# Order of one quarter's modulation columns, and of two loads, at the head of an adaLN linear-attention and GeGLU block

## The chip, the cores and the metric

The kernel runs on one core of one Trainium2 chip. The metric is the device time of one execution in microseconds (us); lower is better. The kernel before takes 838.47 us in the median of its first three runs (838.35 to 839.31).

PE is TensorE, PEld its weight loads, DVE is VectorE, ACT is ScalarE, POOL is GpSimd and SP is SyncE, whose queue issues almost all loads.

## The reference

One transformer block on 2048 tokens of width 1024, in bf16. A conditioning vector `c` makes six modulation vectors. The first two, a shift `sa` and a scale `ca`, are applied to the layer-normalized tokens before the QKV product:

```python
mod = (_silu(c) @ w_mod).reshape(c.shape[0], 6, 1, -1)
sa, ca, ga, sb, cb, gb = ...
h = _layernorm(x) * (1 + ca) + sa
x = x + ga * linear_attention(h, wqkv, wo)     # phi(t) = (t > 0 ? t + 1 : exp(t)) + 1e-6, 32 heads
h = _layernorm(x) * (1 + cb) + sb
x = x + gb * ((gelu(h @ w_gate) * (h @ w_up)) @ w_down)
```

Before any K matmul of a row block of `wk` can run, the matching part of `sa` and `ca` must have been multiplied out, for which 4 MB of `w_mod` are loaded. That head of the kernel is all that matters here.

## The kernel before

Tokens come in chunks of 128. The first four chunks are normalized on DVE (`ln1_bn`, `ln1_fin`, `xhat_dve`), transposed on PE (`t1`) and written to `h1T` by ACT. The modulation is worked out in four quarters of 256 columns; a quarter has two loads of 512 KB, its shift half (t = 0) and its scale half (t = 1). `mod_cols` turns them into four columns of PSUM, with 16 one-column matmuls for a half; `mod_copy` moves them to `modt`; `mod1` applies them to `h1T` on DVE. Then the K matmuls of the two rows of `wk` that belong to the quarter can run.

```python
def wmq_dma(q, ts=(0, 1)):           # shift half first, then scale half
    for t in ts:
        sch.dma(Q, ... WMQ[q][:, :, t, :] <- wm_v[:, :, t * D + q * 256:t * D + (q + 1) * 256] ...)

# the loads, all on SP's queue, in this order
x_dma(0, 1); x_dma(1, 2)
wmq_dma(0, (1,))
x_dma(2, 3)
wmq_dma(0, (0,))
x_dma(3, 4)
w_dma(WK, OFF_WK, "wk", 1, 0, D, 0, 2)               # wk rows 0-1
for q in range(1, 4):
    wmq_dma(q)
    for d0, d1 in ((2, 4),) if q == 1 else ((2 * q, 2 * q + 1), (2 * q + 1, 2 * q + 2)):
        w_dma(WK, OFF_WK, "wk", 1, 0, D, d0, d1)     # wk rows 2-3, 4, 5, 6, 7
w_dma(WV, ...)                                       # ... wv, tokens 4-7, wq

def mod_cols(q, bank, ts=(1, 0)):    # scale columns first, then shift columns
    for t in ts:
        ...                          # 16 matmuls 128x1 for each half

# PE's program order at the head (DVE's parts between)
warm(11, 7); t1(0, 5); warm(6, 7); mod_cols(0, 4); t1(1, 6)
mod_copy(0, 4); mod1(0, 1, 0, 2)
warm(4, 7)                           # matmuls on zeros, filler
k_part(0, [0])                       # K of chunk 0, rows 0-1
xhat_dve(2, ...); t1(2, 7); mod1(1, 1, 0, 2)
ln1_bn(3, 0); ln1_bn(3, 1); ln1_fin(3)
k_part(0, [1])
mod1(2, 1, 0, 2)
mod_cols(1, 4, (1,))                 # quarter 1, scale
k_part(0, [2])                       # K of chunk 2
xhat_dve(3, ...)
mod_cols(1, 4, (0,))                 # quarter 1, shift
mod_copy(1, 4); t1(3, 7); mod1(0, 3, 2, 4)
k_tiles([2, 3], ...)                 # "the next K matmuls": rows 2-3
...
mod_cols(2, 4); mod_copy(2, 4)       # quarter 2
... rows 4-5 ...
mod_cols(3, 4); mod_copy(3, 4)       # quarter 3
... rows 6-7, then the V matmuls (wv)
```

Every operation carries its own waits; an engine runs its list strictly in this order. So a wait of PE for one operand holds all PE work behind it (in the first timeline below, K matmuls that were ready near 15.0 us run at 15.94, behind a wait that ended at 15.52).

Of the kernel before, what the change touches and what calls it, by code (L numbers as in the profile page):

```python
# [12 lines left out]
D = 1024  # L13
# [32 lines left out]
OFF_WK = OFF_WD  # L46
# [168 lines left out]
def bass_adaLN_cond__linear_attn_block__geglu_ffn__prompt_kernel(  # L215
# [15 lines left out]
    with ExitStack() as es:  # L231
# [6 lines left out]
        def at(name, shape, dty, off):  # L238
            return nc.alloc_sbuf_tensor_at(name, shape, dty, offset=ABASE + off, align_bytes=4)
# [10 lines left out]
        WK = at("wk", [P, NDC, D], bf16, OFF_WK)  # L250
# [66 lines left out]
        def r_sm(name):  # L317
            return [(SMO[name], SMO[name] + SMSZ[name], name)]
# [7 lines left out]
        def r_xs(c0, c1):  # L326
            return [(OFF_XALL + c0 * D * 2, OFF_XALL + c1 * D * 2, "xall")]
# [13 lines left out]
        def r_w(off, name, dc, c0=0, c1=D):  # L341
            return [(off + (dc * D + c0) * 2, off + (dc * D + c1) * 2, name)]
# [14 lines left out]
        def r_wmq(i, t):  # L357
            return [(MSO[i] + (dc * 2 + t) * 512, MSO[i] + (dc * 2 + t + 1) * 512, f"wmq{i}") for dc in range(NDC)]
# [33 lines left out]
        def pr(b):  # L392
            return [(b * 2048, (b + 1) * 2048)]

        def PS(b, c0=0, c1=512):
            return ps_all[:, b * 512 + c0: b * 512 + c1]
# [44 lines left out]
        def x_dma(c0, c1):  # L441
            return sch.dma(Q, lambda e: e.dma_start(XALL[:, c0:c1, :], x_v[:, c0:c1, :]), wr=r_xs(c0, c1), note=f"x{c0}")  # L442
# [4 lines left out]
        def w_dma(dst, off, name, kind, c0, c1, dc0=0, dc1=NDC):  # L447
            return sch.dma(Q, lambda e: e.dma_start(dst[:, dc0:dc1, c0:c1], wqkv_v[:, dc0:dc1, kind * D + c0:kind * D + c1]),
                           wr=[t_ for dc in range(dc0, dc1) for t_ in r_w(off, name, dc, c0, c1)], note=f"{name}.{dc0}.{c0}")

        def wmq_dma(q, ts=(0, 1)):
            for t in ts:
                sch.dma(Q, lambda e, t=t: e.dma_start(WMQ[q][:, :, t, :], wm_v[:, :, t * D + q * 256:t * D + (q + 1) * 256]),  # L453
                        wr=r_wmq(q, t), note=f"wmq{q}.{t}")
# [6 lines left out]
        wmq_dma(0, (1,))  # L461
        x_dma(2, 3)
        wmq_dma(0, (0,))
        x_dma(3, 4)
        w_dma(WK, OFF_WK, "wk", 1, 0, D, 0, 2)
        for q in range(1, 4):
            wmq_dma(q)
            for d0, d1 in ((2, 4),) if q == 1 else ((2 * q, 2 * q + 1), (2 * q + 1, 2 * q + 2)):
# [35 lines left out]
        def xhat_dve(c_, dst, rng):  # L504
            sch.op(V, lambda e: e.tensor_scalar(dst[:, :], XALL[:, c_, :], MVA[:, c_, 0:1], RSA[:, c_:c_ + 1],  # L505
                                                op0=ALU.subtract, op1=ALU.mult),
                   rd=r_x(c_) + r_smc("mv", c_, 8) + r_smc("rs", c_, 4), wr=rng, note=f"xhat {c_}")
# [21 lines left out]
        def xh_buf(c_):  # L529
            i = c_ % 3  # L530
            return XH[i], r_2k(XHO[i], f"xh{i}")
# [52 lines left out]
        def mod1(c0, n, dc0=0, dc1=NDC):  # L584
            sg, ci = divmod(c0, CPG)
            mods(H1, r_h1, sg, sc1, ci * P, (ci + n) * P, dc0, dc1, "h1")
# [8 lines left out]
        def mod_cols(q, bank, ts=(1, 0)):  # L595
            o = None
            rng = [(bank * 2048 + (MC0 + q * 4) * 4, bank * 2048 + (MC0 + q * 4 + 4) * 4)]
            for t in ts:
                for b in range(2):
                    col = MC0 + q * 4 + t * 2 + b  # L600
                    for dc in range(NDC):
                        o = sch.op(T, lambda e, t=t, b=b, dc=dc, col=col: e.matmul(  # L602
                            PS(bank, col, col + 1), WMQ[q][:, dc, t, b * P:(b + 1) * P], SILUT[:, dc:dc + 1],
                            start=(q == b == dc == 0 and t == 1), stop=(dc == NDC - 1), skip_group_check=True),
                            rd=r_wmq(q, t) + r_sm("siluT"), pwr=(rng if dc == 0 else ()), note=f"mod{q}.{t}.{b}.{dc}")
            for t_ in rng:
                sch.ps.set_writer(t_[0], t_[1], o)

        def mod_copy(q, bank):
            rng = [(bank * 2048 + (MC0 + q * 4) * 4, bank * 2048 + (MC0 + q * 4 + 4) * 4)]  # L610
            sch.op(V, lambda e: e.tensor_tensor(MODT[:, q * 4:q * 4 + 4], PS(bank, MC0 + q * 4, MC0 + q * 4 + 4), ADD4[:, :], ALU.add),
                   prd=rng, rd=r_sm("add4"), wr=r_smc("modt", q, 16), note=f"modcp{q}")
# [121 lines left out]
        def warm(n, bank=None):  # L734
            for _ in range(n):
                sch.op(T, lambda e: e.matmul(PS(0 if bank is None else bank), WARM[:, 0:P], WARM[:, :], start=bank is not None,
                                             stop=bank is not None, skip_group_check=True),
                       rd=R_WARM, pwr=pr(bank) if bank is not None else (), note="warm")
# [29 lines left out]
        def k_part(q, cs):  # L768
            for dc in (2 * q, 2 * q + 1):
                for (c_, jg), b in kb0.items():  # L770
                    if c_ in cs:
                        kv_mm(c_, "k", jg, b, [dc])
                if 3 in cs:
                    k31([dc])
# [17 lines left out]
        ln1_fin(2)  # L792
        mod_copy(0, 4)
        mod1(0, 1, 0, 2)
        warm(4, 7)
        k_part(0, [0])
        xhat_dve(2, *xh_buf(2))
        t1(2, 7)
# [3 lines left out]
        ln1_fin(3)  # L802
        k_part(0, [1])
        mod1(2, 1, 0, 2)
        mod_cols(1, 4, (1,))
        k_part(0, [2])
        xhat_dve(3, *xh_buf(3))
        mod_cols(1, 4, (0,))
        mod_copy(1, 4)
        t1(3, 7)  # L810
        mod1(0, 3, 2, 4)
# [505 lines left out]
```

## Time and profile before

The page of the kernel before says that PE is busy almost all the time, at full granted clock:

```profile
span 836.2 us, 11354 instructions
PE 829.1 (99%) x4190; PEld 384.3 (46%) x4190; DVE 512.3 (61%) x898; ACT 336.3 (40%) x555; POOL 37.5 (4%) x91
```

The list of PE's waits has four entries (columns: who waited, for whom, us in total, how many times, the longest):

```profile
PE ps_all L478 <- POOL bmask L429: 2.1, 1, 2.1
PE ps_all L602 <- DMA wmq<-in_w_mod_dram: 1.9, 2, 1.0
PE ps_all L680 <- DMA wk<-in_A_wqkv_dram: 0.4, 1, 0.4
PE ps_all L680 <- DVE h1T L565: 0.2, 1, 0.2
```

They all lie before 18.1 us. L602 is `mod_cols`, L680 the K and V matmuls, L565 `mod1`. From there to the end PE waits for nothing, so an advance at the head is kept to the end, if no later load takes it back.

The PE timeline of the kernel before shows the place in question (columns: start, duration, engine, line, operation, tiles and shapes, count, and the idle time before with what ended it):

```profile
12.21 1.02 PE L680 MATMUL ps_all<-wk,h1T 128*128 128x512 bf16 x4 [0.36 <-DMA wk<-in_A_wqkv_dram]
13.07 0.61 PE L546 MATMUL ps_all<-ident,xh 128*128 128x128 bf16 x8
13.52 1.03 PE L680 MATMUL ps_all<-wk,h1T 128*128 128x512 bf16 x4
15.52 0.55 PE L602 MATMUL ps_all<-siluT,wmq 128*128 128x1 bf16 x16 [0.98 <-DMA wmq<-in_w_mod_dram]
15.94 1.02 PE L680 MATMUL ps_all<-wk,h1T 128*128 128x512 bf16 x4
16.80 0.54 PE L602 MATMUL ps_all<-siluT,wmq 128*128 128x1 bf16 x16
18.01 2.55 PE L680 MATMUL ps_all<-wk,h1T 128*128 128x512 bf16 x11 [0.20 <-DVE h1T L565]
21.45 0.94 PE L602 MATMUL ps_all<-siluT,wmq 128*128 128x1 bf16 x32
25.27 0.94 PE L602 MATMUL ps_all<-siluT,wmq 128*128 128x1 bf16 x32
31.00 3.18 PE L680 MATMUL ps_all<-wv,h1T 128*128 128x512 bf16 x14
```

PE stands idle for 0.98 us before the scale columns of quarter 1. Chunk 2's K matmuls, whose operands were ready near 15.0, sit behind them in the list. They run at 15.94, the shift columns after them at 16.80, and the next K matmuls start at 18.01. Quarters 2 and 3 (21.45 and 25.27) wait for nothing, and the V matmuls start at 31.00.

The landing of a load is its issue on SP plus its time to landing, which the views give to 0.1 us, so landings here are good to about 0.05 us. In this profile quarter 1's shift half landed at 6.66 + 7.2 = 13.86, its scale half at 15.48, wk rows 2-3 at 16.92, quarter 2's scale half at 20.29 and quarter 3's at 17.70 + 6.8 = 24.5. These are the SP timeline's line of that last load and the line of the DMA view for it (size and us to landing at the end):

```profile
17.70 1.18 SPq L453 DMA_DIRECT2D wmq<-in_w_mod_dram  x1
wmq<-in_w_mod_dram SPq DMA_DIRECT2D x1, 512.0 KB, 6.8
```

PE came to quarter 3's columns at 25.27, so this load had 0.77 us in hand, in this one execution.

### The profile page before, as it was taken

Reading aid. Unit: us, or ns where it says so; the run is one execution under the profiler, and the core shown is the slowest. Engines: PE = TensorE matmul, PEld = TensorE weight load, DVE = VectorE, ACT = ScalarE, POOL = GpSimd, SP = SyncE. Lnnn points to the kernel's source line nnn. Section 1 sums busy time; section 2 is a strip of 40 time slices with the busy share of each in tenths; the row PEclk is TensorE's granted clock in tenths of the full one; section 3 lists DMA queues with packets and bytes.
Section 4 is the critical chain, followed back from the end, with each engine's and each line's share of the span. In section 5 each row is a group of like instructions: output and inputs, shape, how many; then the busy total and the mean of one; then the engine's idle time right before and its main releaser. Section 6 shows DMA issues by size and latency. Waiting matters only on the chain.

```text
span 836.2 us, 11354 instructions
## 1 busy us (share of the span) xinstructions
PE 829.1 (99%) x4190; PEld 384.3 (46%) x4190; DVE 512.3 (61%) x898; ACT 336.3 (40%) x555; POOL 37.5 (4%) x91
## 2 busy tenths in 40 slices
PE   7999999999999999999999999999999999999998
PEld 4544444444444444444444444444444444444445
DVE  6678877687785567753466665355556535655512
ACT  2357777446423355420444442045554104455300
POOL 2012111000200000000000000000000000000000
PEclk9999999999999999999999999999999999999999
DMA  9984422239696779180555533055553305555000
GB/s 289 322 245 111 92 76 78 76 85 230 143 239 197 227 206 275 26 193 26 158 151 151 152 101 75 20 158 152 151 151 102 76 20 160 152 154 144 7 19 26
DMA packets 184102, 113.22 MB, mean 135 GB/s; under 512 B 35560, under 2 KB 175080, under 8 KB 183024
## 3 DMA queue, kind: packets, MB, share of 16 engines
q1 hardware_dynamic: 184032, 112.50, 50.1%
q8 instruction: 33, 0.54, 0.3%
q14 instruction: 21, 0.17, 0.1%
q10 hardware_dynamic: 16, 0.00, 0.0%
HBM read 100.67 MB, written 4.47 MB: 126 GB/s over the span
## 4 chain that ended last, share of the span: by engine, by line
PE 98%; DMA 1%; SPq 1%; DVE 0%; issue 0%
PE ps_all L1157 23%; PE ps_all L1132 23%; PE ps_all L1129 23%; PE ps_all L680 13%; PE ps_all L1072 7%; PE ps_all L721 7%; DMA wmq<-in_w_mod_dram 1%; PE ps_all L702 1%; SPq L442 0%; PE ps_all L974 0%; PE ps_all L602 0%; PE ps_all L986 0%; PE ps_all L756 0%; SPq L453 0%; PE ps_all L643 0%
## 5 line engine op out<-in xcount | busy, mean ns | idle before, releaser
L1129 PE MATMUL ps_all<-h2T,wg 128*128 128x512 bf16 x896 | 339.6, 379 | 0.0
L1132 PE MATMUL ps_all<-h2T,wu 128*128 128x512 bf16 x896 | 339.6, 379 | 0.0
L1157 PE MATMUL ps_all<-wd,yT 128*128 128x512 bf16 (+3 forms) x952 | 194.2, 366 | 0.0
L1140 ACT ACTIVATE q<-ps_all 128x512 f32<-128x512 f32 x112 | 66.9, 597 | 225.4 <-PE ps_all L1129 221.6
L1157 PEld LDWEIGHTS ps_all<-wd,yT 128*128 128x128 bf16 x952 | 90.1, 98 | 103.9 <-issue 0.4
L1129 PEld LDWEIGHTS ps_all<-h2T,wg 128*128 128x128 bf16 x896 | 87.7, 98 | 105.8 <-issue 0.2
L1132 PEld LDWEIGHTS ps_all<-h2T,wu 128*128 128x128 bf16 x896 | 87.7, 98 | 105.6
L1145 DVE SCALAR_TENSOR_TENSOR ww<-th,guh 128x512 f32<-128x512 f32 x112 | 77.5, 692 | 77.9 <-ACT th L1144 77.9
L1142 DVE SCALAR_TENSOR_TENSOR ww<-q,ps_all 128x512 f32<-128x512 f32 x112 | 76.9, 687 | 77.6 <-ACT guh L1141 77.5
L1144 ACT ACTIVATE th<-ww 128x512 f32<-128x512 f32 x112 | 70.5, 629 | 87.3 <-DVE ww L1142 87.3
L1162 DVE TENSOR_TENSOR ps_all<-ps_all,gbb 128x512 f32<-128x512 f32 (+3 forms) x34 | 22.7, 667 | 94.7 <-PE ps_all L1157 94.6
L1147 DVE TENSOR_TENSOR yT<-ww,ps_all 128x512 bf16<-128x512 f32 x112 | 76.9, 686 | 3.8
L1141 ACT ACTIVATE guh<-ps_all 128x512 f32<-128x512 f32 x112 | 66.3, 592 | 0.0
L721 PE MATMUL ps_all<-h1T,wq 128*128 128x512 bf16 x256 | 58.7, 379 | 0.0
L680 PE MATMUL ps_all<-wv,h1T 128*128 128x512 bf16 x256 | 57.7, 379 | 0.0
L680 PE MATMUL ps_all<-wk,h1T 128*128 128x512 bf16 x248 | 56.6, 379 | 0.6 <-DMA wk<-in_A_wqkv_dram 0.4
L669 ACT ACTIVATE eb<-ps_all 128x512 f32<-128x512 f32 x64 | 37.5, 599 | 48.4 <-PE ps_all L721 21.8
L1072 PE MATMUL ps_all<-w,pq 128*128 128x512 bf16 x256 | 56.2, 379 | 0.0
L670 DVE TENSOR_SCALAR eb<-eb 128x512 f32<-128x512 f32 x64 | 27.1, 423 | 26.1 <-ACT eb L669 25.8
L1072 PEld LDWEIGHTS ps_all<-w,pq 128*128 128x128 bf16 x256 | 25.0, 98 | 30.2 <-issue 0.2
L680 PEld LDWEIGHTS ps_all<-wv,h1T 128*128 128x128 bf16 x256 | 24.9, 98 | 29.5
L680 PEld LDWEIGHTS ps_all<-wk,h1T 128*128 128x128 bf16 x248 | 23.8, 98 | 28.8 <-DVE xh L505 0.8
(96 smaller groups left out, 480.7 us busy)
## 6 DMA issues: line engine op xcount, KB each, us to landing
wg<-in_B_w_gate_dram SPq DMA_DIRECT2D x56, 512.0 KB, 4.1
wu<-in_B_w_up_dram SPq DMA_DIRECT2D x56, 512.0 KB, 5.3
rb<-scr_rd SPq DMA_DIRECT2D x32, 256.0 KB, 7.5
wd<-in_B_w_down_dram SPq DMA_DIRECT2D x7, 1024.0 KB, 8.9
wmst<-in_w_mod_dram SPq DMA_DIRECT2D x6, 1024.0 KB, 6.9
wmq<-in_w_mod_dram SPq DMA_DIRECT2D x8, 512.0 KB, 7.0
out_dram<-xall SPq DMA_DIRECT2D x31, 128.0 KB, 1.7
xall<-in_A_x_dram SPq DMA_DIRECT2D x3, 1024.0 KB, 11.8
```

Of the source, the lines that this page charges most:

```text
L680: o = sch.op(T, lambda e, dc=dc: e.matmul(PS(bank), H1[sg][:, dc, ci * P:(ci + 1) * P], W_[:, dc, jg * 512:(jg + 1) * 512], start=(dc == 0 ...
L721: o = sch.op(T, lambda e, dc=dc: e.matmul(PS(b), WQ[:, dc, qc * P:(qc + 1) * P], H1[sg][:, dc, :], start=(dc == 0), stop=(dc == NDC - 1)), ...
L1072: last[half] = sch.op(T, lambda e, g=g, half=half: e.matmul(PS(b0 + half), PQ[sg][:, g, ci * P:(ci + 1) * P], W2[:, g, half * 512:(half + ...
L1129: og = sch.op(T, lambda e, dc=dc: e.matmul(PS(bg), WG[slot][:, dc, e_ * P:(e_ + 1) * P], H2[sg][:, dc, :], start=(dc == 0), stop=(dc == ND ...
L1132: ou = sch.op(T, lambda e, dc=dc: e.matmul(PS(bu), WU[slot][:, dc, e_ * P:(e_ + 1) * P], H2[sg][:, dc, :], start=(dc == 0), stop=(dc == ND ...
L1140: sch.op(A, lambda e: e.activation(Q1[j][:, :], PS(bg), ACTF.Square, scale=math.sqrt(GELU_A)), prd=pr(bg), wr=rq, note=f"q1 {fc}")
L1141: ogh = sch.op(A, lambda e: e.activation(GUH[j][:, :], PS(bg), ACTF.Copy, scale=0.5), prd=pr(bg), wr=rg, note=f"gh {fc}")
L1142: sch.op(V, lambda e: e.scalar_tensor_tensor(WW[j][:, :], Q1[j][:, :], 1.0, PS(bg), op0=ALU.add, op1=ALU.mult), rd=rq, prd=pr(bg), wr=rw, ...
L1144: sch.op(A, lambda e: e.activation(TH[j][:, :], WW[j][:, :], ACTF.Tanh, scale=GELU_C), rd=rw, wr=rt, note=f"th {fc}")
L1145: sch.op(V, lambda e: e.scalar_tensor_tensor(WW[j][:, :], TH[j][:, :], 1.0, GUH[j][:, :], op0=ALU.add, op1=ALU.mult), rd=rt + rg, wr=rw, n ...
L1147: sch.op(V, lambda e: e.tensor_tensor(YT[:, fc, :], WW[j][:, :], PS(bu), ALU.mult), rd=rw, prd=pr(bu), wr=r_yt(fc), note=f"yT {fc}")
L1157: o = sch.op(T, lambda e, b=b, fc=fc, c0=c0, c1=c1, n=n: e.matmul(PS(b, 0, n), YT[:, fc, ci * P:(ci + 1) * P], WDT[fc // 4][:, fc % 4, c0:c1],
```

## The change

The shift half of a quarter is loaded first and lands first, so its columns are put ahead of chunk 2's K matmuls, and the scale columns behind. In addition, the first wk rows are loaded ahead of the fourth tokens, so that chunk 0's K can start earlier, and one of the four filler matmuls is dropped.

```diff
@@ loads
         wmq_dma(0, (0,))
+        w_dma(WK, OFF_WK, "wk", 1, 0, D, 0, 2)
         x_dma(3, 4)
-        w_dma(WK, OFF_WK, "wk", 1, 0, D, 0, 2)
@@ head
-        warm(4, 7)
+        warm(3, 7)
         k_part(0, [0])
@@ quarter 1
         mod1(2, 1, 0, 2)
-        mod_cols(1, 4, (1,))
+        mod_cols(1, 4, (0,))
         k_part(0, [2])
         xhat_dve(3, *xh_buf(3))
-        mod_cols(1, 4, (0,))
+        mod_cols(1, 4, (1,))
         mod_copy(1, 4)
```

## The prediction

> **What bounds it.** The page gives TensorE (PE) 829.1 of 836.2 us, 99%, at granted clock 1.000; the chain that ended last is 98% PE. The list of PE waits holds four entries, all before 18.1 us: modulation weights (wmq) 1.9 us in two waits, wk 0.4, DVE h1T 0.2, and 2.1 for a mask at the start. So the change can only win in the first 18 us, where the DMA engines are 99% busy, and what is won passes 1:1 to the end unless a later load takes it back. That caps the gain near 2 us, 0.2%.
>
> **The waits now (PE timeline; landing = issue + time to landing).** K of chunk 0 starts at 12.21, when the first wk rows land; the four warm matmuls before it end issuing near 11.7. The scale half of wmq quarter 1 (issued 7.17) lands at 15.48; PE waits 0.98 us for it, although the shift half landed at 13.86 (issued 6.66, 7.2) and chunk 2's K matmuls could start near 15.0 (their h1T is written from 14.78). These run after it, 15.94 to 16.8; shift columns follow, modt is copied at 17.38, and the next K matmuls start at 18.01.
>
> **What the change does.**
> 1. wk rows 0-1 (512 KB) ahead of the fourth tokens (256 KB). At the 322 GB/s of 10.2-12.4 us, 256 KB take about 0.8 us: wk lands about 11.4 instead of 12.2, x3 about 12.2 instead of 10.6. DVE first reads x3 at 12.53, so that costs nothing. The Trainium skill, "DMA: Bandwidth & Descriptors", section "Queues, rings and completion order", says each engine consumes its ring's descriptors in order; the trace agrees, landings follow issue order. Later landings stay put.
> 2. One warm matmul fewer: 0.22 us of filler. K of chunk 0 starts at about 11.5, and h1T of chunk 2 is ready 0.3-0.5 us earlier (14.3-14.5).
> 3. Shift columns (16 matmuls, 0.4 us) run at 13.9, inside what was waiting; K of chunk 2 (4 x 0.216 us) runs 14.6-15.4; the scale columns start at 15.5, holding nothing else up. modt is copied about 16.0 instead of 17.38, h1T is ready about 16.6.
>
> **How much survives.** The next K matmuls need wk rows 2-3, landing at 16.92 (issued 8.72, 8.2): start 16.95, 1.05 us earlier. Then loads set the pace: quarter 2's columns (20.29) just fit, but quarter 3's scale half lands at 24.5 (17.70 + 6.8), and PE, at 25.27 now, would get there at 24.2-24.4 and wait 0.1-0.3 us. Net about 0.75 us. After that wk 7 (25.8), wv (28.1, 29.6, 32.5) and tokens 4-7 (35.3) have 0.4 us or more in hand, and PE is saturated.
>
> **Predicted: 837.7 us** (838.47 - 0.75), 8 in 10 within 836.9 to 838.7. Faster by over 2%: 0.005; within 2%: 0.99; slower by over 2%: 0.005.
>
> **What would show it.** Step 1: PE's wait for wk gone or under 0.1, K of chunk 0 at 11.4-11.6, no new DVE wait over 0.2 for xall. Step 3: 16 column matmuls near 13.9, chunk 2's K before 15.5, modt copy near 16.0. Survival: the K matmuls after quarter 1's copy wait for wk or start near 17.0; a small new PE wait for wmq near 24.4; V begins about 30.3 instead of 31.0.
>
> **What would make it wrong.** Landings shift by some tenths from run to run, the size of the gain itself (before's three runs span 0.96 us). x3 could land after 12.6 and delay DVE's statistics, chunk 2's modulation and chunk 3. If quarters 2 or 3 land later than read here, the gain falls towards zero; if earlier, it reaches 1.05.

## More of the kernel before

The three sets of experiments ran on three different chips (the record doesn't name the chip of the first result), but within a set all kernels ran on the same chip and share the runs of the kernel before. So a difference between sets can be one of chips as well as of executions, and no run here tells the two apart.

## The result, and the profile after

The changed kernel took 838.0 us in the median of six runs (837.6 to 838.2), beside 838.62 us for the kernel before (six runs, 838.35 to 839.31). The ratio is 0.9991 with a 95% interval of 0.9979 to 1.0004: the same, at 2%. A ratio is the mean time of one kernel's fast runs over that of the other's of the same rounds, so it isn't quite the ratio of the quoted medians. The value lies within the predicted range; the interval doesn't exclude 1.

PE's waits in the profile after:

```profile
PE ps_all L478 <- POOL bmask L429: 2.1, 1, 2.1
PE ps_all L602 <- DMA wmq<-in_w_mod_dram: 0.6, 2, 0.4
PE ps_all L680 <- DVE h1T L565: 0.5, 1, 0.5
```

The wait for wk is gone and that for wmq fell from 1.9 to 0.6 us. The PE timeline of the changed kernel, the same places:

```profile
11.47 1.02 PE L680 MATMUL ps_all<-wk,h1T 128*128 128x512 bf16 x4
13.89 0.55 PE L602 MATMUL ps_all<-siluT,wmq 128*128 128x1 bf16 x16
14.42 1.04 PE L680 MATMUL ps_all<-wk,h1T 128*128 128x512 bf16 x4
15.51 0.55 PE L602 MATMUL ps_all<-siluT,wmq 128*128 128x1 bf16 x16
17.02 2.53 PE L680 MATMUL ps_all<-wk,h1T 128*128 128x512 bf16 x11 [0.49 <-DVE h1T L565]
20.57 0.95 PE L602 MATMUL ps_all<-siluT,wmq 128*128 128x1 bf16 x32
24.78 0.95 PE L602 MATMUL ps_all<-siluT,wmq 128*128 128x1 bf16 x32 [0.21 <-DMA wmq<-in_w_mod_dram]
30.51 3.83 PE L680 MATMUL ps_all<-wv,h1T 128*128 128x512 bf16 x17
```

The shift columns run at 13.89, chunk 2's K at 14.42 instead of 15.94, the scale columns at 15.51 as soon as they land, and the next K matmuls at 17.02 instead of 18.01: an advance of 0.99 us. At V only 0.49 us of it are left. The starts show where it went. From the next K matmuls to quarter 2's columns PE took 3.44 us before and 3.55 after, and from there to quarter 3's columns 3.82 before and 4.21 after. So 0.11 us were lost at the landing of quarter 2 and 0.39 at that of quarter 3, although the list of waits shows only 0.21 for the second. What is left at V does reach the end: from V's start to the end of the span it is 805.2 us in both profiles (836.2 - 31.00 and 835.7 - 30.51). The chain of waits names the load: in the kernel before, it ran from 15.5 us to the end through PE, but for some 0.6 us on DVE; now it runs through the issues of SP up to the landing of quarter 3's scale half at 24.74:

```profile
17.27 1.51 SPq L453
18.78 0.04 issue
18.83 5.91 DMA wmq<-in_w_mod_dram
24.73 0.05 issue
24.78 0.95 PE ps_all L602 x32
```

### The profile page after: what moved, and what is told of

The parts are those of the page before. It is cut to its first block, busy times and chain, and to the rows that moved or that the text cites. A ratio compares the mean times of both kernels' runs of the same rounds, so it can differ in the third digit from the quotient of the medians.

```text
span 835.7 us, 11352 instructions
## 1 busy us (share of the span) xinstructions
PE 829.8 (99%) x4189; PEld 384.2 (46%) x4189; DVE 512.3 (61%) x898; ACT 336.2 (40%) x555; POOL 36.7 (4%) x91
## 4 chain that ended last, share of the span: by engine, by line
PE 97%; SPq 2%; DMA 1%; issue 0%; DVE 0%
PE ps_all L1157 23%; PE ps_all L1129 23%; PE ps_all L1132 23%; PE ps_all L680 12%; PE ps_all L1072 7%; PE ps_all L721 7%; SPq L448 1%; PE ps_all L702 1%; SPq L453 1%; DMA wmq<-in_w_mod_dram 1%; PE ps_all L974 0%; PE ps_all L986 0%; SPq L442 0%; PE ps_all L643 0%; PE ps_all L756 0%; PE ps_all L602 0%
```

## The experiments

Twelve entries, of nine different kernels, ran in three sets of four, each with five timed runs. The table gives the medians, that of the kernel before in the same set (nine runs), and the ratio with its interval. No interval excludes 1, so each median is only a hint.

| run | what it is | median us | before, same set | ratio (95%) |
|---|---|---|---|---|
| e0_after | changed kernel again, set 1 | 838.18 | 838.18 | 0.9999 (0.9986 to 1.0011) |
| e1_columns | column order alone, set 1 | 838.86 | 838.18 | 1.0006 (0.9992 to 1.0019) |
| e2_loads | loads and filler alone, set 1 | 838.75 | 838.18 | 1.0005 (0.9992 to 1.0018) |
| e3_q3_shift | changed, quarter 3's shift first too, set 1 | 837.77 | 838.18 | 0.9994 (0.9981 to 1.0007) |
| b1_before | kernel before again, set 2 | 838.63 | 838.33 | 1.0002 (0.9988 to 1.0016) |
| n1_before_free | before, quarters 2 and 3 wait for no load, set 2 | 838.16 | 838.33 | 0.9999 (0.9987 to 1.0012) |
| n2_after_free | changed, the same cut, set 2 | 837.68 | 838.33 | 0.9989 (0.9976 to 1.0001) |
| e5_split_q3 | e3 with wk rows 2 and 3 as two loads, set 2 | 837.86 | 838.33 | 0.9997 (0.9984 to 1.0009) |
| e9_after | changed kernel again, set 3 | 838.77 | 838.31 | 1.0002 (0.9990 to 1.0015) |
| e10_columns | column order alone again, set 3 | 838.16 | 838.31 | 0.9996 (0.9984 to 1.0009) |
| e11_q3_shift | e3 again, set 3 | 838.24 | 838.31 | 0.9998 (0.9985 to 1.0010) |
| e7_loads_fill | e2 with eight filler matmuls in the hole, set 3 | 838.45 | 838.31 | 0.9999 (0.9985 to 1.0012) |

The second table reads one profile of each. "Scale 1" is the start of quarter 1's scale columns, "next K" that of the K matmuls of rows 2-3, L2 and L3 the landings of the scale halves of quarters 2 and 3, "wait 3" the idle time of PE before quarter 3's columns. In the four profiles of set 2 the record of the first of the eleven next K matmuls is missing, so "next K" is read there from the weight load. A dash: not applicable or no wait. In e2 and e5 the granted clock fell for some 3 us before V (see below), which lengthens their steps.

| profile | column order of quarter 1 | scale 1 | next K | next K - scale 1 | L2 | L3 | wait 3 | V starts | V - L3 |
|---|---|---|---|---|---|---|---|---|---|
| before | scale first | 15.52 | 18.01 | 2.49 | 20.29 | 24.50 | - | 31.00 | 6.50 |
| b1_before | scale first | 15.00 | 17.48 | 2.48 | 19.90 | 25.45 | 0.63 | 31.27 | 5.82 |
| e7_loads_fill | scale first | 15.17 | 17.66 | 2.49 | 21.09 | 25.34 | 0.23 | 31.09 | 5.75 |
| n1_before_free | scale first | 15.31 | 17.79 | 2.48 | - | 24.83 | - | 30.78 | - |
| e2_loads | scale first | 15.01 | 18.01 | 3.00 | 19.84 | 24.48 | - | 31.59 | 7.11 |
| after | shift first | 15.51 | 17.02 | 1.51 | 20.51 | 24.73 | 0.21 | 30.51 | 5.78 |
| e0_after | shift first | 14.59 | 16.10 | 1.51 | 20.29 | 24.44 | 0.21 | 30.26 | 5.82 |
| e9_after | shift first | 14.91 | 16.39 | 1.48 | 21.07 | 25.22 | 0.20 | 31.02 | 5.80 |
| e1_columns | shift first | 15.43 | 16.64 | 1.21 | 21.22 | 25.45 | 0.22 | 31.24 | 5.79 |
| e10_columns | shift first | 15.26 | 16.47 | 1.21 | 20.59 | 24.78 | 0.22 | 30.55 | 5.77 |
| e3_q3_shift | shift first | 15.54 | 17.05 | 1.51 | 20.74 | 24.97 | - | 30.37 | 5.40 |
| e11_q3_shift | shift first | 15.07 | 16.59 | 1.52 | 21.07 | 25.21 | - | 30.66 | 5.45 |
| n2_after_free | shift first | 15.50 | 16.95 | 1.45 | - | 25.29 | - | 30.61 | - |
| e5_split_q3 | shift first | 15.12 | 16.34 | 1.22 | 21.21 | 25.39 | - | 32.51 | 7.12 |

My theory after the first result: the advance at quarter 1 is real and fixed at about 1 us, but V can't start earlier than about 5.8 us after L3, and L3 belongs to the loads, not to PE. So the gain is whatever slack the kernel before had at L3. The rival: the change has a fixed gain of about 0.6 us.

### The changed kernel twice more, and the kernel before once more

No edit. The changed kernel:

> The changed kernel once more, as a control for the three runs beside it. Both theories: 0.4 to 0.7 us below the kernel before, V matmuls start at 30.5 +- 0.2 us; this says how far the landings move by themselves.

> The changed kernel a third time, beside the next three. Theory (V starts 5.75 us after quarter 3's scale half lands, or at PE's own pace, whichever is later; landings move by up to 1 us between executions): 0 to 0.6 us below the kernel before, and V in its profile at that landing plus 5.75 within 0.1 us if the list of waits has one for wmq near 24-25 us. Rival (the change has a fixed gain of 0.6 us): 0.6 below.

And the kernel before, in set 2, as a control:

> The kernel before itself, for a profile of it beside the next three. In the last set of runs the changed kernel gained nothing over the kernel before (838.18 both), and quarter 1's scale half landed at 14.6 instead of 15.5. Theory (V starts at the later of PE's own pace and quarter 3's scale landing plus 5.75 us; the gain is the slack that the kernel before has at that landing, 0.77 us in its first profile): where quarter 1's scale lands before 15 here, this kernel too waits for quarter 2's or 3's columns, and V starts within 0.3 us of the changed kernel's. Rival (the kernel before has slack everywhere, the difference is something else): no wait for wmq after 16 us.

In set 1 the changed kernel was level with the kernel before (838.18 both); in set 3 its median was 0.46 us above. The control differed from its own kernel by 0.30 us in the median of set 2. Both runs of the changed kernel missed what was expected of them: 0.4 to 0.7 us below, and 0 to 0.6 below. So the fixed gain of 0.6 us, the rival, was not seen again. The times alone don't exclude it, for 0.6 us is a ratio of 0.9993, which lies inside the intervals of both sets; a difference of medians of 0.3 to 0.5 us in one set is not a result at all. Over all sets the changed kernel's 16 runs have a mean of 838.25 us and the 38 runs of the kernel before 838.44: 0.19 us apart.

The profiles say why. The step from the scale columns of quarter 1 to the next K matmuls is 2.48 to 2.49 us in the old order (3.00 in e2, where the clock fell) and at most 1.52 in the new one, in every profile of the table. That advance is there each time. But L3 was 24.44, 24.73 and 25.22 in three profiles of the changed kernel, and 24.50 and 25.45 in two of the kernel before. The PE timeline of the control has a wait that the first profile of the same kernel hadn't:

```profile
20.92 0.94 PE L602 MATMUL ps_all<-siluT,wmq 128*128 128x1 bf16 x32
25.54 0.95 PE L602 MATMUL ps_all<-siluT,wmq 128*128 128x1 bf16 x32 [0.63 <-DMA wmq<-in_w_mod_dram]
31.27 2.10 PE L680 MATMUL ps_all<-wv,h1T 128*128 128x512 bf16 x9
```

Its SP timeline and DMA view for that load show an issue 0.45 us earlier than in the first profile, but 1.4 us more to landing:

```profile
17.25 1.21 SPq L453 DMA_DIRECT2D wmq<-in_w_mod_dram  x1
wmq<-in_w_mod_dram SPq DMA_DIRECT2D x1, 512.0 KB, 8.2
```

With L3 at 25.45 the kernel before had no slack left, and would have gained nothing at V from an earlier PE. The expectation for the control, that it would start V within 0.3 us of the changed kernel's, can only be held against n2 and e5 of its set, which are other kernels; the new wait was seen as expected. In set 3 the changed kernel met late landings:

```profile
16.39 2.53 PE L680 MATMUL ps_all<-wk,h1T 128*128 128x512 bf16 x11 [0.46 <-DVE h1T L565]
21.09 0.95 PE L602 MATMUL ps_all<-siluT,wmq 128*128 128x1 bf16 x32 [1.12 <-DMA wmq<-in_w_mod_dram]
25.28 0.95 PE L602 MATMUL ps_all<-siluT,wmq 128*128 128x1 bf16 x32 [0.20 <-DMA wmq<-in_w_mod_dram]
31.02 2.32 PE L680 MATMUL ps_all<-wv,h1T 128*128 128x512 bf16 x10
34.85 1.45 PE L680 MATMUL ps_all<-wv,h1T 128*128 128x512 bf16 x6 [0.21 <-DVE pk L672]
```

Its next K matmuls started at 16.39, 1.6 us earlier than in the first profile of the kernel before, and its V at 31.02, no earlier. PE came early to quarter 2's columns and stood there for 1.12 us. It lost a little more behind V: from V's start to the end it is 805.6 us here, not 805.2, and the last line shows a wait of 0.21 us. The last load of wv landed just before it, at 23.70 + 11.1 = 34.8, while the DVE work that the line names ended at 34.66. In e1 and e11 the same stretch is 805.5 and 805.4 us. So V's start isn't the last place where the landings can take something.

### The column order alone, twice

```diff
-        mod_cols(1, 4, (1,))
+        mod_cols(1, 4, (0,))
         k_part(0, [2])
         xhat_dve(3, *xh_buf(3))
-        mod_cols(1, 4, (0,))
+        mod_cols(1, 4, (1,))
```

> The kernel before with only the order of quarter 1's columns changed (loads and the four warm matmuls as before). Theory (the column order makes the gain, and the landing of quarter 3's scale half near 24.7 us caps it): K of chunk 0 stays at 12.2, shift columns at about 14.4, chunk 2's K at about 15.05, the next K matmuls at about 17.0, V at 30.5; 0.5 us below before, the same as the whole change. Rival (the earlier wk rows make the gain, or the two parts add): V at 31.0 or between, gain of at most 0.25 us.

> Only the column order once more; the first time it was 0.7 us slower than the kernel before, with quarter 3's scale half landing at 25.45. Theory (that was a late landing in that placement of the program, not the order): this time no slower than the kernel before by more than 0.3 us, the K matmuls after quarter 1's copy 0.3 to 1.0 us earlier than in the profiles of the kernel before, and V at landing plus 5.75. Rival (the column order without the earlier wk rows is a loss): 0.5 us slower again.

In both profiles the step from the scale columns to the next K matmuls is 1.21 us, as short as in the whole change or shorter (the landing of wk rows 2-3 stretches it there, see below). V started 5.79 and 5.77 us after L3, as the theory has it. The median was 0.68 us above the kernel before in the first set and 0.15 below in the other; in the first set L3 was 25.45 in the profile, in the other 24.78. So the order isn't a loss by itself. The forecast of a gain of 0.5 us in the first of these runs was a miss; its profile has the late landing that the theory names. Since the step is no longer than in the whole change, no run shows that the loads add anything to the new order.

### The loads alone, without and with filler in the hole

```diff
+        w_dma(WK, OFF_WK, "wk", 1, 0, D, 0, 2)
         x_dma(3, 4)
-        w_dma(WK, OFF_WK, "wk", 1, 0, D, 0, 2)
...
-        warm(4, 7)
+        warm(3, 7)
```

> The kernel before with only the wk rows ahead of the fourth tokens and three warm matmuls (column order as before). Theory: K of chunk 0 at 11.5, but the scale columns still wait for their landing at 15.5, now some 1.7 us long, chunk 2's K runs after it at 15.95, the next K at 18.0, V at 31.0; gain 0. Rival: V at about 30.5, gain of about 0.5 us.

Chunk 0's K did start earlier, at 10.86, but the scale columns still held everything up, for 1.81 us, and V started at 31.59, later than in any other profile of the table but that of e5. What had not been expected: after the hole the granted clock of PE fell to 0.50. The PE timeline and the windows view of PE (stretch, its length, PE's busy time and instructions, granted clock, DMA share, GB/s):

```profile
15.01 0.55 PE L602 MATMUL ps_all<-siluT,wmq 128*128 128x1 bf16 x16 [1.81 <-DMA wmq<-in_w_mod_dram]
15.42 1.50 PE L680 MATMUL ps_all<-wk,h1T 128*128 128x512 bf16 x4
```

```profile
14.00:16.00 2.00, 0.99 (x19) 0.96 1.10 340
16.00:19.00 3.00, 3.00 (x30) 0.50 1.19 304
19.00:20.00 1.00, 1.00 (x6) 0.88 1.04 351
```

The four K matmuls took 1.50 us instead of 1.02. To test whether the hole was the cause, eight filler matmuls were put into it:

```diff
+        warm(8)
         mod_cols(1, 4, (1,))
```

> The kernel with the loads alone (wk rows first, three warm matmuls, old column order), with eight warm matmuls more ahead of quarter 1's scale columns, so that TensorE isn't idle for 1.8 us there. In the run without them the granted clock fell to 0.50 from about 15.6 to 19.2 us, and V started at 31.6. Theory (the hole made the clock fall, and that made the loads alone slower than before): clock 1.0 throughout, V at 31.0 or at quarter 3's landing plus 5.75, and about 0.4 us faster than the 0.6 us loss of that run, so level with the kernel before. Rival (the clock fell for another reason, or it cost nothing): still 0.5 us slower, or the clock still at 0.5 in 15-20 us.

The clock stayed at 1.00 in the same stretches:

```profile
14.00:16.00 2.00, 1.91 (x23) 1.00 1.10 344
16.00:19.00 3.00, 2.79 (x34) 1.00 1.19 305
19.00:20.00 1.00, 1.00 (x6) 1.00 0.97 330
```

V started at 31.09, 5.75 us after L3, and the median was 0.14 us above the kernel before instead of 0.57. The mean clock of whole executions says the same: it was 0.998 in three of the five executions of e2 and 1.000 in all five of e7. So the hole is what let the clock fall, though not in every execution, and the loads alone gain nothing: with the old column order an earlier K of chunk 0 only makes the hole longer.

### Quarters 2 and 3 without a wait for their loads

The column matmuls of quarters 2 and 3 read quarter 0's weights, which have long landed. Their outputs are wrong, which doesn't matter for the times. The loads stay, and DVE reads them later.

```diff
-    PS(bank, col, col + 1), WMQ[q][:, dc, t, b * P:(b + 1) * P], SILUT[:, dc:dc + 1],
+    PS(bank, col, col + 1), WMQ[q if q < 2 else 0][:, dc, t, b * P:(b + 1) * P], SILUT[:, dc:dc + 1],
...
+            if c_ == 0:      # after chunk 0's V
+                for q in (2, 3):
+                    for t in (0, 1): ... e.tensor_copy(RDC[:, 0:8], WMQ[q][:, :, t, 0]) ...
```

> The kernel before with quarter 2's and 3's column matmuls reading quarter 0's weights, so that they wait for no load (wrong result on purpose; the loads stay and are read later). Theory: no wait for wmq after 16 us; V at 13.0 us after the K matmuls that follow quarter 1's copy (18.0 then, or 17.1 where the scale half lands at 14.6).

> The changed kernel with the same cut (wrong result on purpose). Theory: with these landings out of the way the change's lead at quarter 1 reaches the end: V again 13.0 us after the K matmuls (about 30.0 with landings as in the first profile), and this is faster than the kernel before with the same cut by the lead at that point, 0.5 to 1.0 us. Rival (the lead is lost to something other than these landings, such as wk rows 4-7 or the evacuation): the gain stays at 0 to 0.5 us, with new waits for wk or DVE after 20 us.

With the cut, the changed kernel's median was 0.48 us below that of the kernel before (837.68 against 838.16), which by itself is no more than such medians move, and its ratio to the uncut kernel before, 0.9989, is the lowest of the table. In the profiles the changed kernel led by 0.84 us at the next K matmuls (16.95 against 17.79) and still by 0.83 at quarter 3's columns (24.23 against 25.06). By V (30.61 against 30.78) the lead had shrunk to 0.17: the next load took the rest. PE timeline of the changed kernel with the cut:

```profile
24.23 0.94 PE L602 MATMUL ps_all<-siluT,wmq 128*128 128x1 bf16 x32
26.77 2.97 PE L680 MATMUL ps_all<-wk,h1T 128*128 128x512 bf16 x12 [0.32 <-DMA wk<-in_A_wqkv_dram]
30.61 0.81 PE L680 MATMUL ps_all<-wv,h1T 128*128 128x512 bf16 x3
```

wk row 7 landed at 22.24 + 4.4 = 26.64, and PE went on at 26.77. The stretch from the end of quarter 3's columns to the last part of K took 4.54 us here (25.03 to 29.57) and 3.88 with the cut in the kernel before (25.86 to 29.74). So both theory and rival of this pair are partly right: without the waits for quarters 2 and 3 the lead passes them whole, as the theory said, and then wk row 7 takes most of it in this profile, which the rival had named. (V 13.0 us after the next K matmuls, as expected of both, came true in the kernel before, 12.99, and not in the changed kernel, 13.66.) It is the whole stream of loads that holds the head. Quarter 3 isn't always the first place where PE meets it, either: in e0, e9, e1 and e10 PE first waited for quarter 2, for 0.63, 1.12, 1.05 and 0.53 us, and the 0.2 us at quarter 3 came after that.

### Quarter 3's shift columns first as well

```diff
-        mod_cols(3, 4)
+        mod_cols(3, 4, (0, 1))
```

> The changed kernel with quarter 3's shift columns ahead of its scale columns too. Theory (PE's last wait, 0.2 us for quarter 3's scale half, caps the gain): PE does the 16 shift columns (0.4 us) while the scale half lands, the wait at 24.6 goes, V starts 0.2 us earlier, 30.3, and the time is 0.2 us below the changed kernel. Rival (something later, the last wk rows or the evacuation, caps it): V stays at 30.5, the wait only moves.

> The changed kernel with quarter 3's shift columns first, once more, beside the changed kernel. Theory: the 0.4 us of shift columns run before the scale half lands, so V starts at that landing plus 5.35 instead of 5.75: 0.2 to 0.4 us below the changed kernel of this set. Rival: equal to it within 0.1 us.

The wait before quarter 3's columns is gone in both profiles, and V starts 5.40 and 5.45 us after L3 instead of 5.75 to 5.82, as expected: the 16 shift columns run while the scale half is on its way. But quarter 3 no longer holds PE in these two profiles: from quarter 2's columns to V they take 9.55 and 9.56 us, which is PE's own pace (9.55 in the first profile of the kernel before), and what PE waited for was quarter 2 (0.18 and 0.93 us). The PE timeline of the second:

```profile
21.10 0.95 PE L602 MATMUL ps_all<-siluT,wmq 128*128 128x1 bf16 x32 [0.93 <-DMA wmq<-in_w_mod_dram]
24.93 0.94 PE L602 MATMUL ps_all<-siluT,wmq 128*128 128x1 bf16 x32
30.66 2.53 PE L680 MATMUL ps_all<-wv,h1T 128*128 128x512 bf16 x11
```

The medians are 0.41 and 0.53 us below the changed kernel of the same sets, and 0.41 and 0.07 below the kernel before. By the times alone it isn't shown to be faster than either; by the profiles it takes about 0.35 us off the way from L3 to V, which makes it the best version with a right result by the profiles, and only by them.

### wk rows 2 and 3 as two loads, with quarter 3's shift first

```diff
-    for d0, d1 in ((2, 4),) if q == 1 else ((2 * q, 2 * q + 1), (2 * q + 1, 2 * q + 2)):
+    for d0, d1 in ((2 * q, 2 * q + 1), (2 * q + 1, 2 * q + 2)):
```

> The changed kernel with quarter 3's shift columns first and wk rows 2 and 3 as two loads. A candidate to beat both. Theory: the K matmuls after quarter 1's copy start when the modulation is written (16.7) instead of at the landing of both rows (16.9-17.0), if row 2 really held them; V still at quarter 3's scale landing plus 5.3 us, about 0.2 to 0.4 us earlier than in the changed kernel. Rival (DVE's modulation alone holds those K matmuls, as the profile's wait says): they stay 0.7 us after the modulation's start.

This asked what holds the next K matmuls in the changed kernel. The profile's wait names DVE, but the modulation starts at 16.30 and its first part is done 0.38 us later; PE starts at 17.02, just after rows 2-3 land at 8.62 + 8.3 = 16.92. In the kernel before, PE starts 0.43 us after the modulation starts (17.58 to 18.01); in the changed kernel, 0.72 us. With two loads it is 0.43 again (15.91 to the weight load at 16.34). So the load of both rows held them, and the wait was put down to the wrong one of two. (The kernel with two loads is compared in one profile, with its first matmul missing. But in e0 and e9 as well the next K matmuls, at 16.10 and 16.39, start just after that load lands, at 7.70 + 8.3 = 16.0 and 8.11 + 8.1 = 16.2.)

It brought nothing at V in the profile: quarter 2's scale half landed at 12.41 + 8.8 = 21.21, PE waited 1.32 us for it, the clock fell to 0.50 from 23 to 26 us, V started at 32.51, 7.1 us after L3 where 5.3 had been expected, and this execution, at 839.89 us, was the slowest of the five. The median is 837.86, 0.47 us below the kernel before in its set, like the 0.41 of e3. The time gained at rows 2-3 was spent waiting at quarter 2.

## Why the prediction was right

| what the prediction said | what the profile after showed |
|---|---|
| wk rows 0-1 land at about 11.4, K of chunk 0 at about 11.5 | 3.68 + 7.7 = 11.38; 11.47 |
| DVE doesn't wait for the later tokens | statistics of chunk 3 at 12.34, no wait |
| shift columns at 13.9, chunk 2's K at 14.6 to 15.4, scale columns at 15.5 | 13.89; 14.42; 15.51 |
| modt copied about 16.0, h1T ready about 16.6 | 16.10; 16.68 |
| next K at 16.95, held by wk rows 2-3 at 16.92 | 17.02, landing 16.92; e5 showed that the load held them |
| quarter 2's columns just fit | 20.57, landing 20.51 |
| PE waits 0.1 to 0.3 us for quarter 3 | 0.21 |
| V at about 30.3 | 30.51 |
| 837.7 us, 0.75 below before | 838.0, 0.62 below before in that set |

The mechanism was right at each step, and the time lay in the range. The match of the wait for quarter 3 is partly one of names: the list shows 0.21 us, but by the starts PE lost 0.39 there, and 0.11 at quarter 2, which was said to just fit. The term that was off in the first result is the landing of quarter 3's scale half: 24.73 instead of 24.5. That took 0.23 us more of the advance and put V 0.2 us later than predicted.

The sentence "Later landings stay put" is the weakest of the prediction. The Trainium skill, "DMA: Bandwidth & Descriptors", section "Queues, rings and completion order", describes descriptors consumed in ring order on each engine, and also says that completion is not first in, first out per issuing engine. The loads looked at here landed in issue order. But order says nothing about the time: L3 lay between 24.44 and 25.45 us over the profiles in the table, a spread of 1.0 us, as large as the advance itself. The slack of 0.77 us that the kernel before had at L3 was one draw. In its second profile it waited 0.63 us there instead. The prediction named this under what would make it wrong, and gave it a range, but still took one trace's slack as the center. That the first set then came out close to this center, 0.62 us below, was in part luck.

The further sets therefore don't confirm a fixed gain of 0.6 us: they gave 0.00 below and 0.46 above. What is shown is the shorter step of about 1.0 us from the scale columns to the next K matmuls, in every profile, and that V starts 5.75 to 5.82 us after L3 wherever PE waits for it at full clock. (That this number is so constant is only PE's own fixed work behind the wait.) That the lost part goes to the landings, of quarter 2, quarter 3, wk row 7 or wv, is shown for the profiled executions; the unprofiled ones have only their times. How large the gain is on average stays open; the pooled means differ by 0.19 us, within what the control moved.

Why the landings move so much stays open too. In the control the loads moved 182 GB/s between 25 and 26 us, where the first profile has 352. But a smaller rate isn't all of it: in e9 the scale half of quarter 2 landed 3.0 us after the shift half, and in the kernel before 1.6, while the core's loads moved 343 GB/s in both stretches. The traces hold a candidate that was not tested: in each profile one 16 KB DMA packet of the kind "instruction" starts between 16.4 and 19.2 us and takes about 1.2 us: at 17.62 in e9, at 18.15 in the first profile of the kernel before, at 19.20 in the control. In e9 it runs just ahead of the stretched landing; in the control wk row 4, whose turn comes after it, landed 2.0 us behind quarter 2's scale half instead of 0.7; in the first profile no landing after it is stretched. That is a coincidence in time, and no run shows that the packet is the cause.

## What to carry to other kernels

Where operands land one by one, let the engine's program order follow the landings, and put nothing that is ready behind a wait for something that isn't: here that shortened the way from quarter 1's last columns to the next matmuls by about 1.0 us every time. Before counting that as a gain, follow the advance to the next load that has to land, and read its slack from several profiles, not from one. And don't shorten the work ahead of a wait that you leave in place: it only makes the hole longer, and here a hole of 1.8 us cost clock as well, in three of five executions.

## What the Trainium skill lacked or had wrong

- "TensorE: Matmul & The Clock Gate", sections "What's actually happening" and "HAM oscillation — how this bites in real kernels": they put the fall of the clock at an idle window of about 3.4 us. Here an idle stretch of 1.81 us, and in another profile one of 1.32 us, were followed by a granted clock of 0.50 for some 3 us; idle stretches of 1.16 and 1.17 us were not. With the 1.81 us hole filled the clock stayed at 1.00. (Two of the five executions with the hole kept a mean clock of 1.000, so a stretch of this length doesn't always do it.)
- The same page, section "Wait — 56ns, not 53.3ns?", gives 215.7 ns from start to start for 512 columns on the warm array. This is no fault, the trace agrees: in the chain of waits of the changed kernel 16 matmuls take 3.45 us, 216 ns each.
- "DMA: Bandwidth & Descriptors", sections "Bandwidth" and "Latency and other measured facts", give rates and latencies but I found no figure for how much a landing moves between executions of one program. Here the same load (quarter 3's scale half) landed at 24.44, 24.73 and 25.22 us in three profiles of one kernel, and took 6.8 and 8.2 us from issue to landing in two profiles of another.
